# Softmax normalised by the transposing products, in the first of four groups of an attention and two MLPs

## The chip, the cores and the metric

The kernel runs on one core of a Trainium2 chip. Its engines work side by side, each through its own queue in order: TensorE (PE, with its weight loads as PEld), VectorE (DVE), ScalarE (ACT), GpSimd (POOL) and SyncE (SP), which here issues all DMAs. The metric is the time of one execution on the device in microseconds; the median of three runs of the kernel before is 675.15 us (674.61 to 675.26).

## The reference

Attention with a window and sinks, then two MLPs, all in 32-bit floats but for the weights, which come as 64-bit floats. There are 2 batches of 8 heads, 768 positions of 64 dimensions; 4 sinks, a window of 128.

```python
scores = scale * np.matmul(q, k.transpose(0, 1, 3, 2))
keep = is_sink | in_window            # first 4 positions, or 0 <= rel < 128
scores = np.where(keep, scores, -1000000000.0)
scores = scores - np.max(scores, axis=-1, keepdims=True)
a = np.exp(scores)
a = a / (np.sum(a, axis=-1, keepdims=True) + 1e-09)
attn_out = np.matmul(a, v)
...
x = attn_out as (1536 tokens, 512)
h = x @ w_in                          # 512 -> 2048, a piecewise square, -> 512
x = g @ w_out
h = x @ w2_in                         # the same with h * relu6(h + 3) / 6
out = g @ w2_out
```

## The kernel before

The tokens are cut in chunks, four for the first MLP and three for the second. The attention is cut in four groups that feed the four chunks of the first MLP; the first group is batch 0, query blocks 0 to 3 of 128 rows. A group has four pairs of heads, and a pair has one unit for each query block, so the first group has 16 units. The first group runs alone ahead of the first MLP product; the later groups are spread between the MLP's products.

A unit goes through five steps. `score` multiplies q by the keys of the block, of the block before it and of the sinks (128, 256 or 260 columns for the blocks 0, 1 and later), one product per head (L325), and DVE adds the mask and takes the row's minimum of the negated scores (L332, into `p` and `nm`). `expo` lets ACT exponentiate and sum the rows (L351, into `p` and `sm`). `normalise` lets DVE add 1e-9 to the sums (L343), take reciprocals (L344) and multiply `p` by them, once per head (L346). `turn` transposes `p` block by block on PE into PSUM (L388, L389), and `sinks` the four sink columns (L400); `copy` brings both to SBUF as `pt` and `pts` (L370). A unit is turned three units behind its score. `mix`, once per pair, multiplies the turned p by v (L425) and splits the result in a high and a low part (L143, L150) for the MLP, whose products read both.

Beside the first group the weights of the first MLP are loaded (`raw`, L173, four buffers), narrowed from 64 to 32 bits (`narrow`: L185 on DVE or L187 on ACT for the absolute value, then L190, L191, L192, L195, L197) and split (L143, L150). The program's order is kept as written on PE and SP; DVE, ACT and POOL follow a scheduler that reckons with its own costs. Where an operation can go to ACT or DVE, a small planner (`Balance`) picks the engine that it reckons to be free first. SP's order matters here: the q and k of the pair after next are issued once a pair's last score is done, and its v once its mix is done; raw weights that come later in the program wait behind them.

Of the kernel before, what the change touches and what calls it, by code (L numbers as in the profile page):

```python
# [8 lines left out]
F32 = mybir.dt.float32  # L9
# [4 lines left out]
ALU = mybir.AluOpType  # L14
AX = mybir.AxisListType

P = 128
# [14 lines left out]

RAW = 4
WO = 5

LAG = 2

# [29 lines left out]
def sink_columns(n_sink):  # L67
    return n_sink + n_sink % 2
# [7 lines left out]
def sink_attention_moe_moe_kernel(  # L76
# [14 lines left out]
    nc = tc.nc  # L91
# [12 lines left out]
    wpool = ctx.enter_context(tc.tile_pool(name="w", bufs=1))  # L104
    wo_p = ctx.enter_context(tc.tile_pool(name="wo", bufs=WO))
    raw_p = ctx.enter_context(tc.tile_pool(name="raw", bufs=RAW))
# [16 lines left out]
    def defer(fn, slots=1):  # L123
        waiting.append((clock[0] + slots, fn))
# [12 lines left out]
    bal = Balance()  # L137
# [26 lines left out]
    ident = consts.tile([P, P], F32, name="ident")  # L164
# [68 lines left out]
    NS = sink_columns(n_sink) if fast else 0  # L233
    KB = P + NS
# [14 lines left out]
    def build_fast_attention(at_p):  # L249
        def key_column(i):  # L250
            return i * P + max(i - 1, 0) * NS
# [18 lines left out]
        pairs = [(gi, hp) for gi in range(len(GROUPS)) for hp in range(H // 2)]  # L270
        col0, at = [], {}
        for ci, _, _, nq in GROUPS:
            col0.append(at.get(ci, 0))
            at[ci] = col0[-1] + nq * P
        qk, vv, probs, pt = {}, {}, {}, {}

        def geom(gi):
            ci, b, i0, nq = GROUPS[gi]
            first = max(i0 - 1, 0)
            return b, i0, nq, first, i0 + nq - first  # L280

        def load(j):

            if j >= len(pairs):
                return
            gi, hp = pairs[j]
            b, i0, nq, first, nb = geom(gi)
            k0, k1 = key_column(first), key_column(i0 + nq - 1) + P
            r0 = 2 * hp * P + D
            tq = at_p.tile([P, NQ * P], F32, tag="qraw", name="qraw")[:, :nq * P]  # L290
            nc.sync.dma_start(out=tq, in_=q[b].rearrange("h r s -> (h r) s")[r0:r0 + P, i0 * P:(i0 + nq) * P])
            tk = at_p.tile([P, KW], F32, tag="kraw", name="kraw")[:, :k1 - k0]
            nc.sync.dma_start(out=tk, in_=k[b].rearrange("h r s -> (h r) s")[r0:r0 + P, k0:k1])
            qk[j] = (tq, tk)
# [17 lines left out]
        def score(j, u):  # L312
            b, i0, nq, first, nb = geom(pairs[j][0])
            tq, tk = qk[j]
            i = i0 + u
            w = widths[min(i, 2)]
            c0 = key_column(max(i - 1, 0)) - key_column(first)
            banks = []
            for e in range(2):
                rows = slice(e * D, (e + 1) * D)  # L320
                if done[0] < ready[0] and u % 2:
                    banks.append(ps_h.tile([P, 512], F32, tag="h", name="ps_s")[:, :w])
                else:
                    banks.append(ps_a.tile([P, 512], F32, tag="a", name="ps_s")[:, :w])
                nc.tensor.matmul(  # L325
                    banks[e], tq[rows, u * P:(u + 1) * P], tk[rows, c0:c0 + w], start=True, stop=True
                )
            p = at_p.tile([P, 2, KB + P], F32, tag="p", name="p", bufs=DIST + 3)[:, :, :w]
            nm = at_p.tile([P, 2], F32, tag="nm", name="nm", bufs=DIST + 2)
            sm = at_p.tile([P, 2], F32, tag="sm", name="sm", bufs=DIST + 2)  # L330
            for e in range(2):
                nc.vector.tensor_tensor_reduce(  # L332
                    out=p[:, e, :], in0=banks[e], in1=masks[min(i, 2)], scale=-SCALE, scalar=BIG,
                    op0=ALU.add, op1=ALU.min, accum_out=nm[:, e:e + 1],
                )
                bal.add("dve", 230 + w / 0.96)
            probs[j, u] = p
            if u == nq - 1:
                qk.pop(j)
                load(j + 2)  # L340

            def normalise():
                nc.vector.tensor_scalar_add(out=sm, in0=sm, scalar1=1e-9)  # L343
                nc.vector.reciprocal(out=sm, in_=sm)  # L344
                for e in range(2):
                    nc.vector.tensor_scalar_mul(out=p[:, e, :], in0=p[:, e, :], scalar1=sm[:, e:e + 1])  # L346
                bal.add("dve", 300 + 2 * (140 + w / 1.92))

            def expo():
                for e in range(2):  # L350
                    nc.scalar.activation(  # L351
                        out=p[:, e, :], in_=p[:, e, :], func=AF.Exp, scale=-1.0, bias=nm[:, e:e + 1],
                        accum_out=sm[:, e:e + 1],
                    )
                bal.add("act", 2 * (480 + w / 1.2))
                defer(normalise)

            defer(expo)

        def bank(name):  # L360

            if not spare:
                return ps_a.tile([P, 512], F32, tag="a", name=name)
            spare.append(spare.pop(0))
            return ps_y.tile([P, 512], F32, tag=f"y{spare[-1]}", name=name)

        def copy(dst, src, n):
            e = bal.pick(act=143 + n / 1.2, dve=140 + n / 0.96)
            if e == "act":
                nc.scalar.activation(out=dst, in_=src, func=AF.Copy)  # L370
            else:
                nc.vector.tensor_copy(out=dst, in_=src)

        def turn(j, u):
            b, i0, nq, first, nb = geom(pairs[j][0])
            i = i0 + u
            if u == 0:
                pt[j] = (
                    at_p.tile([P, 2, NQ, 2, P], F32, tag="pt", name="pt", bufs=2),
                    at_p.tile([NS, 2, NQ, P], F32, tag="pts", name="pts", bufs=2),  # L380
                )
            p = probs[j, u]
            w = widths[min(i, 2)]
            ps = bank("ps_t").rearrange("p (e n q) -> p e n q", e=2, n=2)
            lo = 1 if i == 0 else 0
            for e in range(2):
                if i:
                    nc.tensor.transpose(ps[:, e, 0, :], p[:, e, 0:P], ident)  # L388
                nc.tensor.transpose(ps[:, e, 1, :], p[:, e, w - P:w], ident)  # L389
            copy(pt[j][0][:, :, u, lo:, :], ps[:, :, lo:, :], 2 * (2 - lo) * P)  # L390
            if i < 2:
                probs.pop((j, u))

        def sinks(j, us):

            ps = bank("ps_k").rearrange("p (e u q) -> p e u q", e=2, u=2)
            for n, u in enumerate(us):
                p = probs.pop((j, u))
                for e in range(2):
                    nc.tensor.transpose(ps[0:NS, e, n, :], p[:, e, P:KB], ident)  # L400
            copy(pt[j][1][:, :, us[0]:us[-1] + 1, :], ps[0:NS, :, :len(us), :], 2 * len(us) * P)

        def mix(j):
# [42 lines left out]
        for g in range(len(units) + DIST + MIX_LAG + 1):  # L446
            if g < len(units):
                steps.append(lambda a=units[g]: score(*a))
            while late and late[0][0] <= g:
                j = late.pop(0)[1]  # L450
                steps.append(lambda j=j: mix(j))
                gi, hp = pairs[j]
                ready[GROUPS[gi][0]] = len(steps)
            if 0 <= g - DIST < len(units):
                j, u = units[g - DIST]
                steps.append(lambda a=(j, u): turn(*a))
                b, i0, nq, first, nb = geom(pairs[j][0])
                us = [x for x in range(max(2 - i0, 0), u + 1)]
                if us and (len(us) % 2 == 0 or u == nq - 1):
                    us = us[-2:] if len(us) % 2 == 0 else us[-1:]  # L460
                    steps.append(lambda a=(j, us): sinks(*a))
                if u == nq - 1:
                    late.append((g + 1 + MIX_LAG, j))
# [170 lines left out]
    with tc.manual_schedule(engines={mybir.EngineType.PE, mybir.EngineType.SP}):  # L634
        nc.vector.memset(half, 0.5)
        make_identity(nc, ident)
        with ExitStack() as att:
            if fast:
                at_p = att.enter_context(tc.tile_pool(name="at", bufs=2))
                build_fast_attention(at_p)  # L640
                attend(1)
                load_weights()
                n0 = ready[0]
                while done[0] < n0:
                    attend(done[0] + 1)
                    take_weights(-AHEAD + (AHEAD * done[0]) // n0 - 1)
            else:
                x1_d.append(dram.tile([DM, NT], F32, name="x1_d"))
                dense_attention(x1_d[0])
                load_weights()  # L650
                load_x1(0)
# [75 lines left out]
```

## Time and profile before

| what | value |
|---|---|
| median of 3 runs | 675.15 us |
| the profiled execution | 677.06 us |
| its span, first to last instruction | 675.3 us |
| PE busy | 645.9 us |
| DVE busy | 414.9 us |
| ACT busy | 336.1 us |
| mean granted clock of TensorE | 0.984 |

The profile is of one execution. A timeline lists instructions by their start from the span's beginning; where a row merges several, its count is behind an x, and the time in brackets is the idle time of the engine before it, with what ended it. On PE the record of a product lasts from its start to a modelled end, and the next begins before that; the distance of two starts is what a product costs PE. A granted clock of 1.00 is the higher of TensorE's two levels (2.4 GHz), 0.50 the lower (1.2 GHz).

### The profile page before, as it was taken

The numbers are of one execution on the slowest core, as the hardware profiler recorded it, in microseconds if no ns is written. First come the engines' busy times: TensorE is split into PE (matmuls) and PEld (weight loads), VectorE is DVE, ScalarE is ACT, GpSimd is POOL, SyncE is SP. The second block draws the span as 40 slices with busy tenths as digits, with TensorE's granted clock in tenths as the row PEclk, the third lists the DMA queues.
The fourth block names the chain that finished last, engine by engine and source line by source line (L and its number), as shares of the span: only waits on it lengthen the run. The fifth ranks groups of instructions, "written<-read, shape, count | busy, mean of one in ns | idle before, by whom it ended". The sixth has DMA issues, their size and how long they took to land.

```text
span 675.3 us, 9477 instructions
## 1 busy us (share of the span) xinstructions
PE 645.9 (96%) x3392; PEld 517.0 (77%) x3392; DVE 414.9 (61%) x1031; ACT 336.1 (50%) x711; POOL 3.4 (1%) x19
## 2 busy tenths in 40 slices
PE   6779698999999999999999999999999999999997
PEld 3345476777889898888888878888888888888886
DVE  5979998999666555653789897697232222322222
ACT  6778767757455455554456574574232222322221
POOL 2000000000000000000000000000000000000000
PEclk9978799999999999999999999999999999999999
DMA  7333667664686547152497544993327222152311
GB/s 269 121 119 123 209 214 246 199 184 166 227 292 200 176 158 257 59 189 94 132 404 275 187 156 153 381 360 135 124 82 293 93 94 94 63 194 103 107 65 63
DMA packets 47024, 119.20 MB, mean 177 GB/s; under 512 B 4433, under 2 KB 15745, under 8 KB 46977
## 3 DMA queue, kind: packets, MB, share of 16 engines
q1 hardware_dynamic: 46976, 118.60, 50.5%
q8 instruction: 27, 0.44, 0.3%
q14 instruction: 21, 0.16, 0.1%
HBM read 92.36 MB, written 26.21 MB: 176 GB/s over the span
## 4 chain that ended last, share of the span: by engine, by line
PE 81%; DVE 8%; DMA 6%; ACT 4%; SPq 1%; issue 1%; ACTq 0%
PE ps_h L549 36%; PE ps_y L593 35%; PE ps_v L425 4%; PE ps_s L325 3%; DMA raw0i<-moe_w_in_dram 2%; DMA raw0o<-moe_w_out_dram 2%; DVE w L192 1%; DVE w L197 1%; ACT p L351 1%; PE ps_t L389 1%; PE ps_t L388 1%; PE ps_k L400 1%; ACT w L187 1%; DVE p L332 1%; DMA raw1i<-moe_w_in_dram 1%
## 5 line engine op out<-in xcount | busy, mean ns | idle before, releaser
L593 PE MATMUL ps_y<-gh,wo 128*128 128x512 f32 (+1 forms) x896 | 267.7, 363 | 0.2 <-ACT r L558 0.2
L593 PEld LDWEIGHTS ps_y<-gh,wo 128*128 128x128 f32 x896 | 163.0, 188 | 29.9 <-issue 4.4
L549 PE MATMUL ps_h<-xh,wih 128*128 128x512 f32 (+1 forms) x448 | 166.1, 371 | 7.6 <-DVE gl L150 7.5
L549 PE MATMUL ps_h<-xl,wih 128*128 128x512 f32 (+1 forms) x448 | 161.6, 361 | 0.2 <-DVE xl L150 0.2
L549 PE MATMUL ps_h<-xh,wil 128*128 128x512 f32 (+1 forms) x448 | 161.5, 360 | 0.0
L593 PE MATMUL ps_y<-gl,wo 128*128 128x512 f32 (+1 forms) x448 | 160.7, 359 | 0.0
L150 DVE TENSOR_TENSOR gl<-ps_h,gh 128x512 fp32r<-128x512 f32 (+1 forms) x112 | 68.7, 613 | 87.7 <-ACT gh L143 87.6
L143 ACT ACTIVATE gh<-ps_h 128x512 fp32r<-128x512 f32 (+1 forms) x112 | 59.9, 535 | 108.6 <-PE ps_y L593 86.3
L549 PEld LDWEIGHTS ps_h<-xh,wih 128*128 128x128 f32 x448 | 84.9, 189 | 27.7 <-DVE gl L150 9.4
L549 PEld LDWEIGHTS ps_h<-xl,wih 128*128 128x128 f32 x448 | 85.1, 190 | 12.6 <-DVE xl L150 0.6
L549 PEld LDWEIGHTS ps_h<-xh,wil 128*128 128x128 f32 x448 | 84.8, 189 | 12.9
L593 PEld LDWEIGHTS ps_y<-gl,wo 128*128 128x128 f32 x448 | 84.5, 189 | 12.2
L563 DVE SCALAR_TENSOR_TENSOR ps_h<-r,ps_h 128x512 f32<-128x512 f32 x48 | 33.4, 696 | 85.0 <-ACT r L562 85.0
L562 ACT ACTIVATE r<-ps_h,half 128x512 f32<-128x512 f32 x48 | 33.1, 689 | 88.4 <-PE ps_h L549 88.4
L351 ACT ACTIVATE p<-p,nm 128x260 f32<-128x260 f32 (+2 forms) x96 | 46.5, 484 | 26.3 <-DVE nm L332 25.2
L325 PE MATMUL ps_s<-kraw,qraw 64*128 64x260 f32 (+2 forms) x192 | 41.1, 467 | 10.5 <-DVE nm L332 4.5
L332 DVE CUSTOM_DVE_ANT_0 p<-ps_s,mask 128x260 f32<-128x260 f32 (+2 forms) x96 | 36.4, 400 | 16.0 <-PE ps_s L325 15.7
L558 ACT ACTIVATE r<-ps_h,half 128x512 f32<-128x512 f32 (+1 forms) x64 | 36.6, 573 | 16.2 <-PE ps_h L549 15.6
L559 DVE SCALAR_TENSOR_TENSOR r<-r 128x512 f32<-128x512 f32 (+1 forms) x64 | 35.4, 554 | 15.0 <-ACT r L558 14.8
L190 DVE TENSOR_SCALAR w<-w 128x512 f32<-128x512 f32 x64 | 27.1, 423 | 18.0 <-ACT w L187 17.7
L325 PEld LDWEIGHTS ps_s<-kraw,qraw 64*128 64x128 f32 x192 | 19.5, 214 | 23.1 <-DVE nm L332 8.2
L560 DVE TENSOR_TENSOR ps_h<-ps_h,r 128x512 f32<-128x512 f32 (+1 forms) x64 | 36.0, 562 | 0.8
(59 smaller groups left out, 580.4 us busy)
## 6 DMA issues: line engine op xcount, KB each, us to landing
wo<-wo_d SPq DMA_DIRECT2D x80, 512.0 KB, 3.5
wo_d<-wo SPq DMA_DIRECT2D x32, 512.0 KB, 5.7
raw0i<-moe_w_in_dram SPq DMA_DIRECT2D x16, 512.0 KB, 5.3
raw0o<-moe_w_out_dram SPq DMA_DIRECT2D x16, 512.0 KB, 5.1
raw1i<-moe_w_in_dram SPq DMA_DIRECT2D x16, 512.0 KB, 5.8
raw1o<-moe_w_out_dram SPq DMA_DIRECT2D x16, 512.0 KB, 4.5
xh<-x2h_d SPq DMA_DIRECT2D x3, 1024.0 KB
xl<-x2l_d SPq DMA_DIRECT2D x3, 1024.0 KB, 9.9
```

The costliest lines, as they stand in the source:

```text
L143: nc.scalar.activation(out=dst, in_=src, func=AF.Copy)
L150: nc.vector.tensor_tensor(out=dst, in0=src, in1=f32(hi), op=ALU.subtract)
L325: nc.tensor.matmul(banks[e], tq[rows, u * P:(u + 1) * P], tk[rows, c0:c0 + w], start=True, stop=True)
L332: nc.vector.tensor_tensor_reduce(out=p[:, e, :], in0=banks[e], in1=masks[min(i, 2)], scale=-SCALE, scalar=BIG, op0=ALU.add, op1=ALU.min, a ...
L351: nc.scalar.activation(out=p[:, e, :], in_=p[:, e, :], func=AF.Exp, scale=-1.0, bias=nm[:, e:e + 1], accum_out=sm[:, e:e + 1],)
L549: nc.tensor.matmul(ps, w[:, kc, :], x[:, kc, :], start=i == 0, stop=i == len(ops) - 1)
L558: nc.scalar.activation(out=r, in_=ps, func=AF.Relu, scale=0.5, bias=half)
L559: nc.vector.scalar_tensor_tensor(out=r, in0=r, scalar=1.0, in1=r, op0=ALU.min, op1=ALU.mult)
L560: nc.vector.tensor_tensor(out=ps, in0=ps, in1=r, op=ALU.max)
L562: nc.scalar.activation(out=r, in_=ps, func=AF.Relu, scale=1.0 / 6.0, bias=half)
L563: nc.vector.scalar_tensor_tensor(out=ps, in0=r, scalar=1.0, in1=ps, op0=ALU.min, op1=ALU.mult)
L593: nc.tensor.matmul(ys[dm], a[:, cs], b, start=fc == 0 and i == 0, stop=fc == FC - 1 and i == 2)
```

## The change

In the first group (`DIAG = 1`), `normalise` no longer multiplies p. It makes a tile `dg` with one DVE operation: the identity, for both heads, times the reciprocals, so a diagonal matrix per head. Where p was transposed by the identity, it is now multiplied as an ordinary product with that diagonal as the moving operand: the result is the transposed p with each query's column scaled. The later groups are as before. The planner is told of a lower cost for DVE in these units.

```diff
@@ -32,6 +32,9 @@
 
 RAW = 4
 WO = 5
+
+DIAG = 1
+DG = 3
 
 LAG = 2
 
@@ -272,7 +275,7 @@
         for ci, _, _, nq in GROUPS:
             col0.append(at.get(ci, 0))
             at[ci] = col0[-1] + nq * P
-        qk, vv, probs, pt = {}, {}, {}, {}
+        qk, vv, probs, pt, diags = {}, {}, {}, {}, {}
 
         def geom(gi):
             ci, b, i0, nq = GROUPS[gi]
@@ -328,6 +331,10 @@
             p = at_p.tile([P, 2, KB + P], F32, tag="p", name="p", bufs=DIST + 3)[:, :, :w]
             nm = at_p.tile([P, 2], F32, tag="nm", name="nm", bufs=DIST + 2)
             sm = at_p.tile([P, 2], F32, tag="sm", name="sm", bufs=DIST + 2)
+            diag = pairs[j][0] < DIAG
+            if diag:
+                dg = at_p.tile([P, 2, P], F32, tag="dg", name="dg", bufs=DG)
+                diags[j, u] = dg
             for e in range(2):
                 nc.vector.tensor_tensor_reduce(
                     out=p[:, e, :], in0=banks[e], in1=masks[min(i, 2)], scale=-SCALE, scalar=BIG,
@@ -342,6 +349,14 @@
             def normalise():
                 nc.vector.tensor_scalar_add(out=sm, in0=sm, scalar1=1e-9)
                 nc.vector.reciprocal(out=sm, in_=sm)
+                if diag:
+
+                    nc.vector.tensor_tensor(
+                        out=dg, in0=ident[:, None, :].to_broadcast([P, 2, P]),
+                        in1=sm[:, :, None].to_broadcast([P, 2, P]), op=ALU.mult,
+                    )
+                    bal.add("dve", 300 + 140 + 2 * P / 0.96)
+                    return
                 for e in range(2):
                     nc.vector.tensor_scalar_mul(out=p[:, e, :], in0=p[:, e, :], scalar1=sm[:, e:e + 1])
                 bal.add("dve", 300 + 2 * (140 + w / 1.92))
@@ -370,6 +385,13 @@
                 nc.scalar.activation(out=dst, in_=src, func=AF.Copy)
             else:
                 nc.vector.tensor_copy(out=dst, in_=src)
+
+        def turned(dst, src, j, u, e):
+
+            if (j, u) in diags:
+                nc.tensor.matmul(dst, src, diags[j, u][:, e, :], start=True, stop=True)
+            else:
+                nc.tensor.transpose(dst, src, ident)
 
         def turn(j, u):
             b, i0, nq, first, nb = geom(pairs[j][0])
@@ -385,8 +407,8 @@
             lo = 1 if i == 0 else 0
             for e in range(2):
                 if i:
-                    nc.tensor.transpose(ps[:, e, 0, :], p[:, e, 0:P], ident)
-                nc.tensor.transpose(ps[:, e, 1, :], p[:, e, w - P:w], ident)
+                    turned(ps[:, e, 0, :], p[:, e, 0:P], j, u, e)
+                turned(ps[:, e, 1, :], p[:, e, w - P:w], j, u, e)
             copy(pt[j][0][:, :, u, lo:, :], ps[:, :, lo:, :], 2 * (2 - lo) * P)
             if i < 2:
                 probs.pop((j, u))
@@ -397,7 +419,7 @@
             for n, u in enumerate(us):
                 p = probs.pop((j, u))
                 for e in range(2):
-                    nc.tensor.transpose(ps[0:NS, e, n, :], p[:, e, P:KB], ident)
+                    turned(ps[0:NS, e, n, :], p[:, e, P:KB], j, u, e)
             copy(pt[j][1][:, :, us[0]:us[-1] + 1, :], ps[0:NS, :, :len(us), :], 2 * len(us) * P)
 
         def mix(j):
```

The new operations are L354 (the diagonal) and L392 (the product) of the changed kernel; its other lines stand 3 to 22 lower than before (L332 is L339, L344 is L351, L192 is L195, L197 is L200, L150 is L153, L325 is L328). PE's rows show the first pair's last unit, from its transpositions on. `p_231` and `p_232` are its p, `p_216` and `p_217` that of the unit before, `p_269` that of the next pair's first unit. Before:

```order
L388 MATMUL ps_t_322<-ident_119,p_231 128x128
L389 MATMUL ps_t_322<-ident_119,p_231 128x128
L388 MATMUL ps_t_322<-ident_119,p_231 128x128
L389 MATMUL ps_t_322<-ident_119,p_231 128x128
L400 MATMUL ps_k_341<-ident_119,p_216 4x128 x2
L400 MATMUL ps_k_341<-ident_119,p_231 4x128 x2
L325 MATMUL ps_s_348<-kraw_172,qraw_170 128x260
L325 MATMUL ps_s_350<-kraw_172,qraw_170 128x260
L389 MATMUL ps_t_366<-ident_119,p_269 128x128 x2
```

Now:

```order
L392 MATMUL ps_t_323<-dg_235,p_232 128x128 x4
L392 MATMUL ps_k_341<-dg_220,p_217 4x128 x2
L392 MATMUL ps_k_341<-dg_235,p_232 4x128 x2
L328 MATMUL ps_s_348<-kraw_172,qraw_170 128x260
L328 MATMUL ps_s_350<-kraw_172,qraw_170 128x260
L392 MATMUL ps_t_367<-dg_272,p_269 128x128 x2
```

Every transposition became a product with a `dg`; the order of PE is the same.

DVE's rows show what stands ahead of the same unit's normalisation (`sm_233` and `sm_234` are its sums; `p_292` and `p_315` are units of the next pair, `w32` the narrowed weights). Before:

```order
L191 TENSOR_SCALAR raw0i2_182<-raw0i2_182 128x512
L332 ISA p_292,nm_293<-ps_s_290,mask1_131 128x256
L332 ISA nm_293 128x1
L197 ISA w32_330<-raw0i1_180,w32_330 128x1024
L344 RECIPROCAL sm_233<-sm_233 128x2
L192 SCALAR_TENSOR_TENSOR w32_418<-w32_418,raw0i2_182 128x512
L150 TENSOR_TENSOR wil0_0_253<-w32_254,wih0_0_252 128x512
L332 ISA p_315,nm_316<-ps_s_311,mask2_132 128x260
L332 ISA nm_316 128x1
L343 TENSOR_SCALAR sm_271<-sm_271 128x2
L346 TENSOR_SCALAR p_231<-p_231,sm_233 128x260 x2
```

Now, up to the diagonal:

```order
L195 SCALAR_TENSOR_TENSOR w32_418<-w32_418,raw0i2_182 128x512
L351 RECIPROCAL sm_234<-sm_234 128x2
L350 TENSOR_SCALAR sm_271<-sm_271 128x2
L339 ISA p_292,nm_293<-ps_s_290,mask1_131 128x256
L339 ISA nm_293 128x1
L153 TENSOR_TENSOR wil0_1_330<-w32_331,wih0_1_329 128x512
L339 ISA p_315,nm_316<-ps_s_311,mask2_132 128x260
L339 ISA nm_316 128x1
L200 ISA w32_418<-raw0i2_182,w32_418 128x1024
L339 ISA p_315,nm_316<-ps_s_313,mask2_132 128x260
L339 ISA nm_316 128x1
L354 TENSOR_TENSOR dg_235<-ident_119,sm_234 128x256
```

The wil of `w32_331`, the second L339 of `p_315` and the L200 of `w32_418` stand ahead of the normalisation now; before, they stood behind it. The first weight's absolute value has also moved from ACT (L187) to DVE (L188 of the changed kernel).

## Rows read from the trace of the kernel before

**Rows 1.** The head and the first part of the page: busy us (share) xinstructions.

```profile
span 675.3 us, 9477 instructions
...
PE 645.9 (96%) x3392; PEld 517.0 (77%) x3392; DVE 414.9 (61%) x1031; ACT 336.1 (50%) x711; POOL 3.4 (1%) x19
```

**Rows 2.** Busy times by stage, all engines; columns as the first line says.

```profile
core 0: us, PE busy (x) PEld busy (x) DVE busy (x) ACT busy (x) POOL busy (x), PEclk, DMA share, GB/s
4.50:64.80 60.30, 48.94 (x241) 26.57 (x241) 51.81 (x211) 47.29 (x132) 0.00 (x0) 0.89 0.47 154
64.80:147.00 82.20, 73.61 (x351) 53.92 (x350) 77.92 (x185) 59.13 (x124) 0.00 (x0) 0.96 0.63 209
```

**Rows 3.** Waits of PE, 4.5 to 64.8 us: us in total, times, longest.

```profile
PE ps_t L388 <- DVE p L346: 4.9, 4, 2.6
PE ps_s L325 <- DVE nm L332: 4.5, 3, 1.8
...
PE ps_v L425 <- ACT pts L370: 1.9, 2, 1.3
```

**Rows 4.** The chain of waits in order of time: start us, us, what.

```profile
17.51 0.60 DVE w L197
...
18.78 0.60 DVE wil L150
19.38 0.34 DVE p L332
...
24.61 4.25 PE ps_v L425 x20
...
42.15 4.17 DMA raw0i<-moe_w_in_dram
```

**Rows 5.** Timeline of PE: start us, us, operation, count, idle before.

```profile
20.12 0.47 PE L388 MATMUL ps_t<-ident,p 128*128 128x128 f32 x1 [2.56 <-DVE p L346]
20.39 0.42 PE L389 MATMUL ps_t<-ident,p 128*128 128x128 f32 x1
20.60 0.42 PE L388 MATMUL ps_t<-ident,p 128*128 128x128 f32 x1
...
28.77 0.45 PE L388 MATMUL ps_t<-ident,p 128*128 128x128 f32 x1
...
31.50 0.27 PE L389 MATMUL ps_t<-ident,p 128*128 128x128 f32 x1
31.60 0.27 PE L388 MATMUL ps_t<-ident,p 128*128 128x128 f32 x1
...
59.67 0.30 PE L388 MATMUL ps_t<-ident,p 128*128 128x128 f32 x1 [0.72 <-DVE p L346]
...
62.53 0.65 PE L425 MATMUL ps_v<-pts,vs 4*64 4x256 f32 x4
63.11 1.73 PE L425 MATMUL ps_v<-pt,vraw 128*64 128x256 f32 x16
```

**Rows 6.** The score's line L325, all: ns min/median/max, first and last start, forms.

```profile
L325 PE MATMUL ps_s<-kraw,qraw x192: 272/480/800, 4.5 to 297.5; 64*128 64x260 f32 x128, 64*128 64x128 f32 x32, 64*128 64x256 f32 x32
```

**Rows 7.** Busy times over the third mix and the group's end; columns as rows 2.

```profile
52.20:56.40 4.20, 4.20 (x20) 2.00 (x20) 4.20 (x18) 3.62 (x11) 0.00 (x0) 0.50 0.01 2
57.00:64.70 7.70, 6.97 (x53) 4.02 (x52) 6.80 (x34) 6.69 (x19) 0.00 (x0) 1.00 0.60 184
```

**Rows 8.** Timeline of DVE; columns as rows 5.

```profile
14.87 0.62 DVE L346 TENSOR_SCALAR p<-p,sm 128x260 f32<-128x260 f32 x2
15.40 0.69 DVE L192 SCALAR_TENSOR_TENSOR w<-w,raw0i 128x512 int32<-128x512 int32 x1
...
22.67 0.47 DVE L346 TENSOR_SCALAR p<-p,sm 128x128 f32<-128x128 f32 x2
...
47.09 0.43 DVE L190 TENSOR_SCALAR w<-w 128x512 f32<-128x512 f32 x1 [2.00 <-ACT w L187]
...
96.09 0.42 DVE L150 TENSOR_TENSOR xl<-ps_v,xh 128x256 fp32r<-128x256 f32 x1
96.42 0.69 DVE L560 TENSOR_TENSOR ps_h<-ps_h,r 128x512 f32<-128x512 f32 x1
```

## The prediction

> **What bounds the kernel now.** The page's first part gives the whole: PE is busy for 645.9 of 675.3 us [rows 1], so whatever ends the part ahead of PE's full load sooner or later shows in the time. The busy times by stage say where PE isn't full [rows 2]: from 4.5 to 64.8 us, the attention of the first group, PE is busy 48.94 of 60.30 us and DVE 51.81; from there to 147 us DVE is busy 77.92 of 82.20 us, as it narrows and splits the weights. Behind that the change touches nothing.
>
> The waits of PE in the first stage come next [rows 3]: 4.9 us on p's normalisation, 4.5 on the row minima, 1.9 on the copied sinks, 11.3 in all. They look like room for more PE work. The chain of waits says how much of it is room [rows 4]: it leaves DVE at 20.1 us, stays on PE until the first pair's mix ends at 28.86 (the piece of 4.25 us from 24.61), then goes through SP, where v and behind it the raw weights are issued, over ACT to the next load of raw weights at 42.15. So PE's work between 20.1 and 28.86 us lies on the path; what PE does from there to 56.4 us, where the third mix ends, lies mostly beside ACT and DMA.
>
> **The products.** A score product at L325 is an ordinary one of 32-bit numbers, and the trace has 192 records of its 96, two each [rows 6]. A transposition has one. In the first group 72 transpositions become ordinary products: per pair 2 + 3 x 4 of blocks and 4 of sinks, in four pairs. I price the second record as the first. Transpositions start 0.21 us apart at 20.39 and 20.60 us, and 0.10 at 31.50 and 31.60, half of it [rows 5]. These are TensorE's two levels, 1.2 and 2.4 GHz: the granted clock over the mix at 52.2 us is 0.50, over 57.0 to 64.7 us 1.00 [rows 7]; from 20.1 us I go by the starts. Bounds for one at the lower level: nothing, if the second record hid, and 0.42 us, if a load of weights as long as the record stood bare beside it. I take 0.21, the row.
>
> The page "FP8 and Floating Point Precision" of the Trainium skill (TensorE Precision Notes) speaks for more: true FP32 takes four passes through the array. With three further passes instead of one, the ten products named next would cost 6.3 us and not 2.1. The records here show two for each product [rows 6], and no row shows four.
>
> **On the path, 20.1 to 28.86 us.** There stand ten of them: four of the first pair's last unit, four of sinks, two of the next pair. At the lower level 10 x 0.21 = 2.1 us more.
>
> **DVE.** Two multiplications at 260 columns take 0.53 us of DVE (14.87 to 15.40), in a row of 0.62; two at 128 columns have a row of 0.47, so 0.38 by the same overlap of 0.09 [rows 8]. I take 256 columns as 260. The diagonal is one TENSOR_TENSOR of 128x256, which the trace has at L150 with 0.33 us (96.09 to 96.42) [rows 8]. Its operands there are not broadcast; bounds 0.27 (half of 0.53) and 0.60 (a 128x512 one [rows 4]); I take 0.33. So DVE is rid of 4 x (0.05 + 3 x 0.20) = 2.6 us. The planner now gives DVE the first weight's absolute value: 0.34, as L190 at 47.09 (0.43 less 0.09) [rows 8]. 2.3 us net.
>
> But DVE's order moves too, and that PE sees. Ahead of the first pair's last normalisation now stand three instructions that stood behind it: a wil at L150 (0.60), an L332 of 260 columns (0.34), an L197 (0.60), 1.54 us [rows 4]. The absolute value adds 0.34, two units' normalisation saves 0.40. PE, which began at 20.12 after a wait of 2.56 us [rows 5], begins 1.5 us later. Bounds: nothing, if DVE can run ahead, and 1.9 without the saving.
>
> **The clock on that path.** PE rests 1.5 us longer and then has 2.1 us more to do without a break. The mix takes 4.25 us at the lower level and 2.3 at the higher (62.53 to 64.84 [rows 5]). The rise stood at the mix's very end, between 28.77 and 31.50 [rows 5]; now more work stands before it. Bounds of the gain: 0 and 2.0 us, the whole mix; I take the middle, 1.0.
>
> **From the first mix to the end of the group.** The mix ends 1.5 + 2.1 - 1.0 = 2.6 us later, and with it the raw weights come to ACT 2.6 us later. The second and third pairs' other 34 products and the last pair's first two cost 0.1 to 0.2 us each, about 5 us; beside them stand PE's waits on row minima and sinks, 4.5 + 1.9 us [rows 3]: nothing, and up to 2 us if that cover is gone. The last pair's other 16, between 56.4 and 61 us, are at the higher level, with 0.72 us of wait there (59.67 [rows 5]): 16 x 0.105 - 0.72 = 1.0 us. DVE's saving in that part is three units' 0.20, so -0.6. Sum: 2.6 + 1.0 - 0.6 = 3.0 us at the group's end.
>
> **After the group.** DVE carries 95% up to 147 us [rows 2], so a late start passes on; but 4.3 us of idle are left there, and the scheduler has put DVE's and ACT's work in another order in part of it: bounds -2.1 and +2.1, half the idle time either way. I take a quarter of it as absorbed, -1.1. Total 3.0 - 1.1 = +1.9 us. The profiled execution took 677.06 us with a span of 675.3; the runs have a median of 675.15, and a difference of spans passes to it as it is: 677.1 us.
>
> **Rivals.**
> 1. The clock comes up and stays; faster. As a mechanism of this kernel: the ten products cost 1.1 us and not 2.1, the first mix 2.0 less, the score and transpositions ahead of it about 1.0 less (half of the 2 us or so that they hold), the third mix, at 0.50 now [rows 7], 2.0 less: 1.5 + 1.1 - 2.0 - 1.0 - 2.0 + 1.0 - 0.6 = -2.0, so 673.2 us. For it: behind the transpositions at 20.12 to 20.60 us the clock stayed low until 28.77 [rows 5]. Against it: the third mix follows on waits for ACT, which remain. The page "TensorE: Matmul & The Clock Gate" of the Trainium skill (Part 4: PE-mode transpose) states the rule behind this case, that a transposition doesn't count as PE-busy in the same way; no row here sets the two kinds side by side.
> 2. DVE decides; faster. The doubled records lie in the 11.3 us of waits [rows 3], and DVE, nearly full through both stages [rows 2], is rid of 2.3 us: 672.9 us. For it is DVE's load; against it that DVE itself waits for raw weights, 2.00 us at 47.09 [rows 8], and those follow PE.
> 3. Slower by more. PE's longer rest before 21.6 us holds the clock low through the mix, the cover of the middle pairs is short by 1 us, and nothing is absorbed: 1.9 + 1.0 + 1.0 + 1.1 = +5.0, 680.2 us.
> 4. Nothing measurable. The normalisation isn't late, since DVE runs ahead, and the clock's 1.0 is there: 1.9 - 1.5 = +0.4, 675.6 us.
>
> **How the numbers follow.** About 0.2% (1.35 us) is what a measurement of this kernel tells from no change. Forecast 0.45, with a range of its own from +0.6 to +3.6 (675.8 to 678.8), its lower end within 0.2%; the clock 0.17; DVE 0.12; slower by more 0.12; nothing 0.14. Faster by over 0.2%: nearly all of the clock and DVE cases, 0.27. Slower by over 0.2%: 0.43 + 0.12 = 0.55. Within: 0.18. The range goes from 672.4, just under the DVE case, to 680.6, just over the third rival.
>
> **What would show it.** Right: 144 records at the new product's line; PE's wait before the first pair's fourth unit ends near 21.6 us; the first mix ends near 31.5 us, the last near 67.8 (64.84 now). Wrong: products of the new kind 0.1 us a record before 25 us, and mixes of 2.3 us throughout (rival 1); the last mix done before 63 us (rival 2); more than two records a product.

## The result, and the profile after

The changed kernel takes 684.07 us (median of three runs, 680.89 to 685.84) where the kernel before took 675.15: a ratio of 1.0122 with an interval of 1.0091 to 1.0153, so 8.9 us slower where 1.9 were forecast. The profiled execution took 685.84 us, with a span of 684.1: 8.8 more than in [rows 1].

The head and the first part of its page:

```profile
span 684.1 us, 9618 instructions
...
PE 654.1 (96%) x3464; PEld 527.4 (77%) x3464; DVE 413.8 (60%) x1016; ACT 335.7 (49%) x710; POOL 3.4 (0%) x19
```

72 PE records more, as many as products were made of transpositions, and 8.2 us more of PE. By stage, with the columns of [rows 2]:

```profile
4.50:64.80 60.30, 50.60 (x275) 33.71 (x276) 46.76 (x179) 42.62 (x120) 0.00 (x0) 0.86 0.43 141
64.80:147.00 82.20, 71.41 (x343) 50.89 (x341) 76.00 (x186) 59.44 (x125) 0.00 (x0) 0.94 0.63 205
```

In the second window, which now begins with the group's last 4.8 us, PE is busy 2.2 us less than before and DVE 1.9 less: both wait more. What PE waits for in the first group (in total, times, longest), to be read against [rows 3]:

```profile
PE ps_v L447 <- ACT pts L385: 5.7, 2, 3.2
PE ps_s L328 <- DMA kraw<-k_dram: 4.3, 1, 4.3
PE ps_t L392 <- DVE sm L351: 3.7, 1, 3.7
```

The wait on row minima (4.5 us before) is gone but for 0.2, and the sinks, 1.9 us before, now hold PE for 5.7. The timeline of PE, against [rows 5]:

```profile
21.60 2.05 PE L392 MATMUL ps_t<-dg,p 128*128 128x128 f32 x8 [3.73 <-DVE sm L351]
23.58 1.87 PE L392 MATMUL ps_k<-dg,p 128*4 128x128 f32 x8
25.38 1.24 PE L328 MATMUL ps_s<-kraw,qraw 64*128 64x260 f32 x4
...
28.02 0.65 PE L447 MATMUL ps_v<-pts,vs 4*64 4x256 f32 x4
28.59 1.73 PE L447 MATMUL ps_v<-pt,vraw 128*64 128x256 f32 x16
30.26 1.16 PE L392 MATMUL ps_t<-dg,p 128*128 128x128 f32 x8
31.35 0.70 PE L328 MATMUL ps_s<-kraw,qraw 64*128 64x256 f32 x4
...
54.57 1.00 PE L447 MATMUL ps_v<-pts,vs 4*64 4x256 f32 x4 [3.21 <-ACT pts L385]
55.50 3.26 PE L447 MATMUL ps_v<-pt,vraw 128*64 128x256 f32 x16
...
69.63 0.50 PE L571 MATMUL ps_h<-xh,wih 128*128 128x512 f32 x1
```

The diagonal comes at 21.60 us, as forecast. Eight records (four products) then take 1.98 us at the lower level, 0.25 each, and 1.09 at the higher one (30.26 to 31.35), 0.14 each; 0.21 and 0.105 were priced. The first mix now runs at the higher level (1.73 and not 3.26), the third still at the lower. The MLP's first product starts at 69.63; in the kernel before the last mix, begun at 63.11 [rows 5], ends with that product's start at 64.77. So 4.9 us are lost at the group's end, and 3.9 of the 8.8 behind it.

Behind the group PE's instructions are the same, in the same order, in both kernels, so each can be compared with its twin. The changed kernel is 4.9 us late at the MLP's first product, 2.8 at a product that starts at 115.81 us before, 8.0 at a transposition that starts at 124.97, and 8.8 at the end. So 5.3 us are lost between these two, 2.1 were made up ahead of them and 0.7 are lost behind. PE of the changed kernel there:

```profile
118.58 0.50 PE L615 MATMUL ps_y<-gh,wo 128*128 128x512 f32 x1
...
119.84 0.40 PE L615 MATMUL ps_y<-gh,wo 128*128 128x512 f32 x1
122.51 0.50 PE L571 MATMUL ps_h<-xh,wih 128*128 128x512 f32 x1 [2.28 <-DVE gl L153]
...
124.42 0.63 PE L571 MATMUL ps_h<-xh,wil 128*128 128x512 f32 x1
124.98 1.11 PE L447 MATMUL ps_v<-pts,vs 4*64 4x256 f32 x4
126.03 1.97 PE L447 MATMUL ps_v<-pt,vraw 128*64 128x128 f32 x12
...
133.01 0.60 PE L394 MATMUL ps_t<-ident,p 128*128 128x128 f32 x4
```

and the same instructions in the kernel before:

```profile
115.81 0.50 PE L593 MATMUL ps_y<-gh,wo 128*128 128x512 f32 x1
...
119.15 0.65 PE L425 MATMUL ps_v<-pts,vs 4*64 4x256 f32 x4 [0.28 <-DVE nm L332]
119.73 1.09 PE L425 MATMUL ps_v<-pt,vraw 128*64 128x128 f32 x12
...
124.97 0.27 PE L388 MATMUL ps_t<-ident,p 128*128 128x128 f32 x1
```

From the first of these rows to the last it is 14.43 us now and 9.16 before. PE waits 2.28 us for gl (the low part of the MLP's inner result; gh is the high part), and behind that wait products take 0.63 us where they took 0.39, and the mix 3.1 where it took 1.7: about 3.0 us more. gl is late because of where DVE has it, and ACT its input gh. DVE runs without a break here:

```profile
119.55 0.62 DVE L361 TENSOR_SCALAR p<-p,sm 128x260 f32<-128x260 f32 x2
120.08 0.42 DVE L193 TENSOR_SCALAR w<-w 128x512 f32<-128x512 f32 x1
120.42 0.42 DVE L194 TENSOR_SCALAR raw0o<-raw0o 128x512 int32<-128x512 int32 x1
120.75 0.69 DVE L581 SCALAR_TENSOR_TENSOR r<-r 128x512 f32<-128x512 f32 x1
121.35 0.28 DVE L339 CUSTOM_DVE_ANT_0 p<-ps_s,mask 128x128 f32<-128x128 f32 x1
...
121.77 0.69 DVE L153 TENSOR_TENSOR gl<-ps_h,gh 128x512 fp32r<-128x512 f32 x1
```

and ACT:

```profile
118.78 0.68 ACT L580 ACTIVATE r<-ps_h,half 128x512 f32<-128x512 f32 x1
119.35 0.60 ACT L146 ACTIVATE gh<-ps_h 128x512 fp32r<-128x512 f32 x1
```

The kernel before, DVE and ACT:

```profile
115.86 0.69 DVE L150 TENSOR_TENSOR gl<-ps_h,gh 128x512 fp32r<-128x512 f32 x1 [0.21 <-ACT gh L143]
...
117.07 0.62 DVE L346 TENSOR_SCALAR p<-p,sm 128x260 f32<-128x260 f32 x2
...
118.80 0.29 DVE L332 CUSTOM_DVE_ANT_0 p<-ps_s,mask 128x128 f32<-128x128 f32 x1
```

```profile
115.24 0.59 ACT L143 ACTIVATE gh<-ps_h 128x512 fp32r<-128x512 f32 x1
...
116.80 0.69 ACT L558 ACTIVATE r<-ps_h,half 128x512 f32<-128x512 f32 x1
```

Before, gl started as soon as gh was there (115.83), ahead of p<-p,sm and of the row minima, and gh stood ahead of r. Now r is ahead of gh on ACT, and gl starts 1.8 us after gh's end (119.95), behind p<-p,sm and the row minima. The changed source touches none of these instructions; the scheduler, which simulates the engines' times, put them in another order.

### The profile page after: what moved, and what is told of

Same layout as the page of the kernel before. It is cut to its first block, busy times and chain, and to the rows that moved or that the text cites. A ratio compares the mean times of both kernels' runs of the same rounds, so it can differ in the third digit from the quotient of the medians.

```text
span 684.1 us, 9618 instructions
## 1 busy us (share of the span) xinstructions
PE 654.1 (96%) x3464; PEld 527.4 (77%) x3464; DVE 413.8 (60%) x1016; ACT 335.7 (49%) x710; POOL 3.4 (0%) x19
## 4 chain that ended last, share of the span: by engine, by line
PE 74%; DVE 10%; DMA 9%; ACT 4%; issue 1%; SPq 1%; ACTq 0%
PE ps_h L571 32%; PE ps_y L615 32%; PE ps_v L447 4%; DMA raw0i<-moe_w_in_dram 4%; PE ps_s L328 2%; DMA raw0o<-moe_w_out_dram 2%; DMA raw1i<-moe_w_in_dram 2%; DVE w L195 2%; DVE w L200 2%; PE ps_t L394 2%; DMA raw1o<-moe_w_out_dram 1%; ACT w L190 1%; DVE wil L153 1%; ACT p L366 1%; DVE gl L153 1%
## 5 line engine op out<-in xcount | busy, mean ns | idle before, releaser
L153 DVE TENSOR_TENSOR gl<-ps_h,gh 128x512 fp32r<-128x512 f32 (+1 forms) x112 | 68.7, 613 | 87.4 <-ACT gh L146 87.2
L339 DVE CUSTOM_DVE_ANT_0 p<-ps_s,mask 128x260 f32<-128x260 f32 (+2 forms) x96 | 36.7, 400 | 18.8 <-PE ps_s L328 18.6
L328 PE MATMUL ps_s<-kraw,qraw 64*128 64x260 f32 (+2 forms) x192 | 37.9, 452 | 4.9 <-DMA kraw<-k_dram 4.3
L385 ACT ACTIVATE pt<-ps_t 128x512 f32<-128x512 f32 (+1 forms) x48 | 26.6, 553 | 11.0 <-PE ps_t L394 5.5
```

What stands on the lines that cost most here:

```text
L153: nc.vector.tensor_tensor(out=dst, in0=src, in1=f32(hi), op=ALU.subtract)
L328: nc.tensor.matmul(banks[e], tq[rows, u * P:(u + 1) * P], tk[rows, c0:c0 + w], start=True, stop=True)
L339: nc.vector.tensor_tensor_reduce(out=p[:, e, :], in0=banks[e], in1=masks[min(i, 2)], scale=-SCALE, scalar=BIG, op0=ALU.add, op1=ALU.min, a ...
```

## Experiments

The ratios are those to the kernel before, run beside each. One table for all, from the profiled executions: the MLP's first product and the span against the kernel before (64.77 and 675.3 us), what lies between the two shifts, the wait for gl and the mix near 119 us, and the time of the stretch around them (the products from 115.81 to 124.97 us of the kernel before, 9.16 us there). Each shift is that of one execution: 28 executions of the kernel before beside e1 to e4 lie between 671.7 and 678.6 us, and its profiled one was 1.9 us above its median. The stretch is the surer sign, since it is short and the same in all.

| kernel | median us | ratio (interval) | first MLP product | span | lost behind the group | wait for gl, mix | stretch |
|---|---|---|---|---|---|---|---|
| changed, first profile | 684.07 | 1.0122 (1.0091-1.0153) | +4.9 | +8.8 | +3.9 | 2.28, 1.11 + 1.97 | 14.43 |
| e1 changed, again | 683.45 | 1.0125 (1.0096-1.0154) | +1.7 | +5.0 | +3.3 | 2.14, 1.11 + 1.97 | 14.34 |
| e2 products alone | 678.72 | 1.0047 (1.0022-1.0072) | +1.2 | +0.9 | -0.3 | 0.91, 0.65 + 1.09 | 9.99 |
| e3 diagonal, not read | 676.78 | 1.0028 (1.0011-1.0045) | -5.8 | -0.6 | +5.2 | 2.31, 1.12 + 1.98 | 14.48 |
| e4 diagonal, transposed with | 674.71 | 1.0001 (0.9984-1.0018) | -3.4 | -2.8 | +0.6 | none, 0.65 + 1.09 | 8.78 |
| e7 float32r | 672.32 | 0.9956 (0.9931-0.9981) | +3.6 | -5.5 | -9.1 | none, 0.65 + 1.09 | 8.76 |
| e8 old price | 678.38 | 1.0055 (1.0025-1.0085) | -1.4 | +1.9 | +3.3 | 2.17, 1.12 + 1.98 | 14.35 |

**e1, the changed kernel again.**

> The changed kernel once more, against the one before. If the +8.9 us is the kernel's own, the median comes to 681 to 686 us and the first product of the MLP stands near 69.6 us again (64.8 before). If a good part of it was the chip's state on one day (its three runs lay 5 us apart), it comes to 677 to 680. The trace also tells which part comes back each time: the group (+4.9 us) and what lies behind it (+4 us).

683.45 us: the loss is the kernel's own. The part behind the group came back (+3.3 us, with a wait of 2.14 us at the same place). The part in the group did not come back whole: +1.7. The second mix waited 1.51 us for its sinks and not 2.47, and ran at the higher level (1.73 us at 39.21; 2.80 at 40.58 in the first profile). The third mix again waited 3.19 us for the sinks and ran at the lower level.

**e2, the products alone.**

```
-    nc.tensor.matmul(dst, src, diags[j, u][:, e, :], start=True, stop=True)
+    nc.tensor.matmul(dst, src, ident, start=True, stop=True)
     (normalise: p multiplied as before, no diagonal)
```

> The products alone: the first group's 72 transpositions are ordinary products with the identity, p is multiplied on VectorE as before, no diagonal is made. Theory (records cost 0.245 us at the lower level and 0.137 at the higher, and the late diagonal costs 1.5 us apart from that): the first mix ends 1 to 2 us later than before, the group's end comes 2.5 to 3.5 us later, the whole 678 to 682 us. If PE's records alone made the loss: group's end +4.9, the whole 683 to 685. If the late diagonal alone made it: within 1 us of the kernel before.

678.72 us, inside the theory's range, but not by its way: the first mix ended 1.6 us earlier than before, where the theory had 1 to 2 later, and the group's end, +1.2, is less than its 2.5 to 3.5. Two mixes ran at the higher level (25.46 and 38.34 us, 1.73 each) that had run at the lower. The median is 0.5% slower, though in the profiled executions only 0.9 us show; where the rest lies isn't known.

**e3, the diagonal made and not read.**

```
-    nc.tensor.matmul(dst, src, diags[j, u][:, e, :], start=True, stop=True)
+    nc.tensor.transpose(dst, src, ident)
```

> The VectorE part alone: the diagonal is made in place of the multiplications, but the transpositions stay transpositions with the plain identity and don't read it, so the first group's p is left without its normalisation, and nothing waits for the diagonal. Theory: PE is no later than before at 20 us (it waits for the exponentials only), the group's end comes 0 to 2.5 us earlier than before, the whole 672 to 676 us. If what VectorE does (a changed order, other picks of the planner) made the loss behind the group: group's end as before and the whole 678 to 682 us.

676.78 us, 0.8 above the theory's range. The group ended 5.8 us earlier, more than the 2.5 I allowed, and all but 0.6 of that was lost behind it, with gl late at the same place (2.31 us). So behind the group the other theory is right, though not in that the group stays as it was.

**e4, transposed with the diagonal.**

```
-    nc.tensor.matmul(dst, src, diags[j, u][:, e, :], start=True, stop=True)
+    nc.tensor.transpose(dst, src, diags[j, u][:, e, :])
-    op=ALU.mult          (diagonal)
+    op=ALU.is_ge
```

> The diagonal's wait without the doubled records: the diagonal is made at the same place by the same form of instruction, with a comparison in place of the product, so that it holds ones, and the transpositions stay transpositions but read it; the first group's p is so left without its normalisation. PE waits for the diagonal as in the changed kernel and has one record for each transposition. Theory: PE begins the first pair's last unit 0.5 to 1.5 us later than before, the group's end comes 0.5 to 1.5 us later, the whole 675.5 to 678. If the records made all of the loss: 674 to 676 and nothing late at the group's end. If the late diagonal made all of it: group's end +4 to +5 and the whole 681 to 684.

674.71 us. PE began at 21.54, 1.4 us late as in the changed kernel, and the group still ended 3.4 us earlier than before. So the wait for the diagonal alone doesn't make the loss; that it costs nothing isn't shown, since the group of e3, which doesn't wait, ended 2.4 us earlier still. "The records made all of the loss" fits this run in its number, but e6 below takes it away. The two halves, e2 and e3, make 0.47% and 0.28%, less than the whole's 1.25%; each of these kernels has its own order of DVE and ACT.

**e5 and e6, a pair under a plain scheduler.** Both kernels with one word changed, so that DVE's and ACT's order no longer comes from simulated times; PE's and SP's orders are written out in the kernel and stay.

```
-    with _tile.TileContext(nc, schedule_with_timeline_sim=True) as tc:
+    with _tile.TileContext(nc, schedule_with_timeline_sim=False) as tc:
```

> The kernel before, with VectorE's and ScalarE's instructions ordered by a scheduler that doesn't simulate the engines' times. It is one half of a pair with the next run, and its own time is not forecast closely: 665 to 690 us. gl comes earlier among VectorE's instructions than in the kernel before (by 4 to 12 us of work up to 147 us), so if a late gl costs PE time between 65 and 147 us, PE's waits for gl shrink there below the 7.2 us of before.

> The changed kernel under the same plain scheduler. From the fourth gl on VectorE's order is the same in both kernels of the pair, so what differs behind the group is only what the group hands on. Theory (behind the group it is the changed order that loses 4 us): the group's end comes 1 to 4 us later than in the pair's other kernel and the difference stays or shrinks behind it; the whole is 0 to 3 us slower than the other. If a late group by itself made the loss behind it (a late transfer, a clock that falls): the difference grows by 3 us or more between 65 and 150 us, and the whole is 5 us or more slower than the other.

The kernel before takes 674.84 us (0.9987, 0.9959 to 1.0014), the changed one 670.46 (0.9932, 0.9908 to 0.9956). Neither theory had that: with the order of the MLP's work the same in both, the change is 4.4 us faster, and faster than both kernels of the question. Its group ends at 54.66 us, the other's at 57.86; behind it the difference grows further in its favour, to 5.8 us of span (1.4 of it because the first one's profiled execution was that much above its median). Of the waits for gl between 64.8 and 150 us (7.2 and 9.0 us under the other scheduler) 1.1 is left in the first of the pair and none in the second. Other waits took their place: 6.9 and 8.8 us on row minima, 0.3 in the kernel of the question. So the kernel before begins the MLP 6.9 us earlier under the plain scheduler and is no faster. Busy times of the kernel before under the plain scheduler, 15 to 55 us (columns as [rows 2]):

```profile
15.00:25.00 10.00, 8.36 (x43) 4.63 (x43) 9.37 (x40) 8.87 (x24) 0.00 (x0) 0.71 0.49 165
25.00:35.00 10.00, 8.62 (x54) 4.95 (x52) 7.59 (x33) 7.95 (x22) 0.00 (x0) 0.84 0.37 108
35.00:45.00 10.00, 8.83 (x44) 4.47 (x44) 8.41 (x36) 9.63 (x27) 0.00 (x0) 0.84 0.38 126
45.00:55.00 10.00, 9.43 (x52) 5.08 (x50) 9.21 (x38) 9.32 (x26) 0.00 (x0) 0.84 0.58 179
```

and of the changed kernel under it:

```profile
15.00:25.00 10.00, 10.00 (x70) 7.02 (x68) 8.32 (x39) 8.60 (x25) 0.00 (x0) 1.00 0.33 102
25.00:35.00 10.00, 9.81 (x78) 6.71 (x76) 9.75 (x42) 10.00 (x32) 0.00 (x0) 1.00 0.54 171
35.00:45.00 10.00, 9.93 (x78) 6.56 (x74) 9.76 (x40) 10.00 (x30) 0.00 (x0) 1.00 0.53 160
45.00:55.00 10.00, 10.00 (x77) 6.69 (x74) 9.56 (x38) 10.00 (x28) 0.00 (x0) 1.00 0.49 154
```

PE is busy nearly throughout and its clock stays at 1.00, where the other falls to 0.71 and 0.84. The four mixes take 1.73 us each behind their sinks, in the other 3.25, 2.35, 3.26 and 3.25. This is the first rival's mechanism, on another order.

**e7, one record instead of two.**

```
-    dg = at_p.tile([P, 2, P], F32, tag="dg", ...)
+    dg = at_p.tile([P, 2, P], F32R, tag="dg", ...)     (p of the first group as well)
```

> The changed kernel with p and the diagonal of the first group kept as float32r, so that the products with the diagonal need one record and not two. The scheduler counts them cheaper too, and puts gl 4.5 to 6 us of work earlier among VectorE's instructions. Theory: the first group ends no later than before plus 1 us, gl isn't late at 118 us, and the whole is 670 to 676 us. If the wait for the diagonal alone were the cost: group's end +3 or more and the whole 680 or more.

672.32 us, as the theory had it, but not by its way: the group ended 3.6 us late, more than the 1 allowed (its four mixes took 3.05 to 3.26 us), and the gain came behind it, 9.1 us. Of these, 7.6 lie between 70 and 85 us of the kernel before, which waits 6.00 us there for another gl, at 77.92; e7 waits 0.96, at 76.16. Over the whole program this kernel and the changed one have the same instructions on DVE and ACT, and PE's order is the same, but DVE's and ACT's is another: the gl near 119 us starts after 93.0 us of DVE's busy time, where it has 100.4 ahead of it in the changed kernel and 98.7 before, and PE's waits for gl from 64.8 to 150 us are 1.5 us where they were 9.0. So the loss behind the group goes with the order. That order alone is worth it isn't shown: DVE had also done 53.6 us of work by the MLP's first product, and 50.8 in the changed kernel.

**e8, the planner told the old price.**

```
-    bal.add("dve", 300 + 140 + 2 * P / 0.96)
+    bal.add("dve", 300 + 2 * (140 + w / 1.92))
```

> The changed kernel with the planner told the old price of the normalisation, so that the first weight's absolute value stays on ScalarE; VectorE's order behind the group has gl as late as in the changed kernel (1.9 us of work later than before, where 2.2 stood). Theory: the loss behind the group stays, 679 to 684 us in all. If the picks of the planner were the cause: 674 to 677.

678.38 us, 0.6 under the theory's range and over the other's. The loss behind the group stayed at 3.3 us, with gl as late, so the picks weren't the cause of that part. But over half of the whole loss is gone (+0.55%, and +1.25% in e1; the intervals don't meet), and it went from the group, which ended 1.4 us earlier than before: PE waited 2.75 us for the diagonal and not 3.73, and the first two mixes ran at the higher level. So in the group the planner's price, with the order that follows from it, does matter.

**e9 and e10, the two halves under the plain scheduler.** The edits of e2 and e4.

> The products alone under the plain scheduler: ordinary products with the identity in the first group, p multiplied on VectorE as before. Two theories of why the change is 4.4 us faster under this scheduler. A, the ordinary products keep the clock up: the granted clock in the first group is 0.95 or more here too (0.83 in the plain kernel before), its mixes take 2.3 us and not 4.3, and the MLP begins within 3 us of the 54.7 us of the changed plain kernel, or earlier than the 57.9 of the plain kernel before. B, VectorE's relief does it: the clock stays low as in the plain kernel before, and the MLP begins at 58 to 61 us.

> The diagonal without the ordinary products, under the plain scheduler: the diagonal holds ones, and transpositions read it, so the first group's p is left without its normalisation. A (the ordinary products keep the clock up): the granted clock falls in the first group as in the plain kernel before, some mixes take 4.3 us, and the MLP begins at 55.5 to 59 us though PE has 72 records less. B (VectorE's relief): PE doesn't wait, the clock stays up, and the MLP begins at 50 to 54 us.

The products alone: 670.67 us (0.9926, 0.9904 to 0.9949), the whole gain. The clock is 1.00 from 15 to 55 us, and the MLP begins at 52.87. The diagonal with transpositions: 673.22 us (0.9962, 0.9936 to 0.9989), clock 0.87, two mixes at 3.25 us, MLP at 58.24. Theory A holds. VectorE's relief is worth 1.6 us at most beside transpositions (674.84 to 673.22, with intervals that overlap) and nothing that can be told beside products (670.67 to 670.46).

**e11 and e12, one record under the plain scheduler.** The edit of e7, and in e12 the diagonal in all groups:

```
-DIAG = 1
+DIAG = 9
```

> The changed kernel under the plain scheduler with p and the diagonal as float32r: the order on every engine is the one of the changed plain kernel, and 72 products have one record and not two. At 0.137 us a record, that is up to 9.9 us less of PE between 16 and 53 us. If the second records are on the path there, the MLP begins 2 to 8 us earlier than at 54.7 us; behind it VectorE decides until 147 us, so the whole is 666 to 671 us. If the second records cost nothing because PE has no more than VectorE: the MLP begins at 54 to 55 us and the whole is the same 670. If a shorter record lets the clock fall: mixes of 4.3 us and 672 to 676.

> The same with the diagonal in all groups, not in the first alone: VectorE is rid of the other groups' multiplications too, between 85 and 320 us, and PE's transpositions there become single-record products of about the same length. Theory: VectorE decides up to 147 us, so 1 to 3 us come back there and nothing behind it, where PE decides: 664 to 670 us. If a float32r product is longer than a transposition and PE decides: 671 to 676.

675.92 us (1.0015, 0.9994 to 1.0036) and 675.06 (1.0002, 0.9982 to 1.0023): the third case for e11, the second in its number for e12, both slower than e6 with less work. e12's mixes all take 3.25 us, and its MLP begins at 64.92, e11's at 60.34. e11 has the order of e6 on every engine, and 72 records fewer. PE in e6 (two records a product), 13 to 24 us:

```profile
13.32 1.19 PE L392 MATMUL ps_t<-dg,p 128*128 128x128 f32 x4 [5.11 <-DVE sm L350]
14.45 0.80 PE L328 MATMUL ps_s<-kraw,qraw 64*128 64x128 f32 x4
15.18 2.07 PE L392 MATMUL ps_t<-dg,p 128*128 128x128 f32 x8
...
17.18 0.70 PE L328 MATMUL ps_s<-kraw,qraw 64*128 64x256 f32 x4
...
23.87 1.73 PE L447 MATMUL ps_v<-pt,vraw 128*64 128x256 f32 x16
```

and in e11 (one record):

```profile
13.34 0.66 PE L392 MATMUL ps_t<-dg,p 128*128 128x128 f32 x2 [5.15 <-DVE sm L350]
13.92 0.80 PE L328 MATMUL ps_s<-kraw,qraw 64*128 64x128 f32 x4
14.65 1.11 PE L392 MATMUL ps_t<-dg,p 128*128 128x128 f32 x4
15.70 1.23 PE L328 MATMUL ps_s<-kraw,qraw 64*128 64x256 f32 x4
...
24.10 3.18 PE L447 MATMUL ps_v<-pt,vraw 128*64 128x256 f32 x16
```

Both start after the same wait, and neither waits up to its first mix. The scores of 256 columns, the same instructions in both, take 0.70 us in one and 1.23 in the other: with two records a product the clock is up by 17 us, with one it is down through the mix. e11 has less to do and yet reaches the mix at 24.10 us, e6 at 23.87. Its granted clock is then 0.50 from 35 to 45 us.

## Why the prediction was wrong

**The direction was right, the size was not: +8.9 us for +1.9.** Of the steps, in their order:

- *The second record.* Two records a product, as priced, and no four. Each takes 0.25 and 0.14 us, not 0.21 and 0.105: the ten products on the path took 4.8 us (eight records in 1.98 us, eight in 1.80, four in 1.04 from 26.55), where their ten transpositions had taken 2.5 (20.12 to 22.02 and 23.19 to 23.81): 2.3 us more, near the 2.1 forecast, since a transposition too cost more than its inner distance of 0.21.
- *The late normalisation*, +1.5: PE begins at 21.60 and not 20.12, exactly so in the first profile, 1.0 in e1. The diagonal costs DVE the 0.33 us priced (21.04 to 21.37). But e4 has the same late start, and its group still ends earlier than before.
- *The clock on that path*, -1.0: it gave back 2.0 us on the first mix (4.2 to 2.2), the whole of its bound, and 0.3 on the score ahead of it. The mix ended 1.5 us late (1.5 + 2.3 - 2.3), not 2.6.
- *From the first mix to the group's end*, +0.4 forecast: +3.4 in the first profile, +0.6 in e1. What differs most is the second mix: it waits 2.47 and 1.51 us, and with the transpositions behind it it takes 4.4 (40.58 to 44.95) and 3.0 (39.21 to 42.21). The third waited 3.2 us for its sinks in both (0.62 before), and the products that "stand beside waits" took the place of one wait (row minima) only to meet another. Nor does the first mix's end decide the group's, as the sum has it: in e4 the mix ended 1.4 us late and the group 3.4 early, in e2 1.6 early and 1.2 late. This term has no one size; it hangs on the waits and on the clock behind them.
- *After the group*, -1.1: this is the step that failed. I saw that the scheduler had put DVE's and ACT's work in another order and took it as half the idle time either way, then as a small gain. It was +3.9 and +3.3 us. What it had wrong is that a new order was priced by DVE's idle time; it costs what PE waits for a result that now comes later, and the slow clock behind that wait. At the one gl near 119 us that is 2.3 us of wait and 3.0 of slower products. In the four profiles of the table where PE waits 2.1 to 2.3 us for this gl, the stretch around it takes 14.3 to 14.5 us; in the three others, and before, 8.8 to 10.0. In the four, ACT has r ahead of gh; in the others gh is ahead of r. The net loss behind the group is 3.3 to 5.2 us in the four and 0.6 at most in the others. A kernel that moves only this gl back wasn't tried, and why the scheduler chose this order isn't known. In e1, e3 and e8 gl starts 1.1, 0.6 and 0.6 us after gh's end, and gh itself ends after PE has begun to wait, so how the lateness is shared between DVE and ACT differs.

The third rival's +5.0 us is nearer only by luck: it too adds nothing behind the group, and it has the clock low through the first mix, which ran at the higher level.

**What the prediction gave 0.17 and should have followed further** is the first rival's mechanism. It is there, and the order decides whether it comes through: with ordinary products and no wait over 1.24 us from 15 to 55 us the clock is 1.00 there and the mixes take 1.73 us (e6, e9); e2, with the same products as e9 but another order, waits 2.85 and 2.82 us and has slow products behind both; in the changed kernel PE waits 3.7, 2.5 and 3.2 us in the group, and behind each of these waits products come to run at the lower level. The page "TensorE: Matmul & The Clock Gate" of the Trainium skill (Part 4: PE-mode transpose) says that a transposition doesn't count as PE-busy in the same way. The pair e9 and e5 agrees, 1.00 and 0.71 to 0.84; they differ in the kind of product in the first group and in some of DVE's and ACT's order there. Not every ordinary product does it: with those of one record (e11) the clock didn't rise where it did with two (e6).

## What to carry to other kernels

Where an order comes from a simulation of times, a change of one group's cost reorders work far behind it; look for the results that the bounding engine waits for (gl here) in the new order, and price each that moved back by more than its slack, and the slow stretch behind it. Before judging an edit, run both kernels also under a scheduler that leaves the work behind it in place: here the sign turned from +8.9 to -4.4 us. That order needn't be the better one: the kernel before took the same time under both. More work on PE can be less time, if it keeps the clock at its higher level.

## What was not expected of the hardware

- A float32r product of 128 columns has one record, yet four of them take 1.05 us at the lower level (14.65 to 15.70, e11) where four transpositions took 0.91 (20.12 to 21.03, before).
- The clock column reads 1.00 for 15 to 25 us in e11, where scores take 1.23 us and the mix 3.18, as at the lower level elsewhere; it also reads 1.00 up to 45 us in e12, whose first two mixes take 3.25. Where the two differ, the lengths of like products say more than the column.
- The clock fell behind waits of 2.1 to 2.3 us near 119 us in four profiles, and stayed up behind one of 0.91 (e2).
